# Block-sparse attention with an FFN: gathering the neighbour K blocks beside the sampled ones, and striding the sampled rows over the partitions

## The chip, the cores and the metric

The kernel runs on one core of one Trainium2 chip. The metric is device time in microseconds (us). The engines are named as the profile names them: PE (TensorE, the matmuls), PEld (its weight loads, which overlap PE), DVE (VectorE), ACT (ScalarE), POOL (GpSimd) and SP (SyncE, which here only issues DMAs).

## The reference

Attention over 4 batches, 8 heads, 768 positions and 64 dimensions, with a mask of 24 x 24 blocks of 32 positions, and behind it a feed-forward layer with the activation h - tanh(h):

```python
mask = np.abs(blk_i - blk_j) <= window          # window = 1
mask = mask | (blk_i == 0) | (blk_j == 0) | (blk_i == n_blocks - 1) | (blk_j == n_blocks - 1)
for qb in range(n_blocks):
    for kb in sampled_blocks[qb]:               # 3 drawn blocks for each query block
        mask[qb * block:(qb + 1) * block, kb * block:(kb + 1) * block] = True
scores = np.where(mask, scale * q @ k.T, -1000000000.0)
attn = softmax(scores)
x = (attn @ v) moved to (3072, 512)
out = (h - np.tanh(h)) @ w_out   with   h = x @ w_in
```

Query blocks 0 and 23 see all keys. Each of the 22 others sees eight blocks of keys: itself with its two neighbours (96 keys), the first and the last block (64) and three sampled ones (96). A sampled block that repeats one of the others counts once; the kernel turns the V rows of such a repeat to zeros, so its keys drop out.

## The kernel before

The heads are worked in two passes (`c` = 0 and 1) of four heads. A pass has 30 units: eight for query blocks 0 and 23 (kinds Y and X) and 22 of kind `block`, one for each other query block with its four heads and four batches. 44 block units in all, and they are what the change touches. K and Q of a pass stand turned in SBUF (`kq`): 128 partitions are two heads of 64 dimensions each.

A block unit `n` goes through these steps:

- `gather_k` (lines 207 to 210), on POOL: three copies of 128 partitions x 8 x 32 elements, from columns of `kq` that a register gives (`bass.ds(x, 32)`), into the tile `kr`, whose 160 columns are block 0, three sampled blocks, block 23. The two fixed blocks are put there once a pass (`edges_k`). There are `NKR` = 2 such tiles, so the copies for unit n wait for the scores of unit n - 2.
- `gather_v` (lines 217 to 226), on the SP queue: one DMA of 96 rows for the neighbours into `vw[..][0]`, and three of 32 rows for the sampled blocks into partitions 0:32, 32:64 and 64:96 of `vw[..][1]`; a row is 4,160 bytes. Partitions 96:128 of both hold the fixed blocks (`edges_v`). There are `NVW` = 4 such pairs of tiles; the gather for unit n waits for `accum` of unit n - 4.
- `scores` (lines 231 to 248), on PE: for two halves of the heads, four batches (`q`) and two heads in the rows of the array (`j`), one product of 96 columns straight from `kq` and one of 160 columns from `kr`, so 32 matmuls a unit. In float32 the profile counts each as two matmul instructions with a weight load each.
- `most` on DVE (row maxima), `exps` on ACT, `turn` on PE (8 transposes), `copy` out of PSUM on ACT and DVE, `accum` on PE (32 matmuls of 65 columns with V), `norm` on DVE, and a DMA of the result to DRAM (`xscr`).

What stands when is written out by hand: every step has a time in units (`at(n + 0.3, scores, u)`, line 358), all are sorted by it, and each engine and the SP queue keep that order. The gathers have theirs here:

```python
at(n - NKR + 0.35, gather_k, u)
at(n - NVW + 2.65 if u.i >= NVW else -3.5, gather_v, u)
at(n + 0.3, scores, u)
```

In the first pass the SP queue also carries the K, Q and V of the second (`load_kq` at 9.5, 11.5, 13.5, 15.5, `load_vnat` at 16, 18, 20, 22), in the second the first weights of the FFN. The FFN follows from about 329 us on.

Of the kernel before, what the change touches and what calls it, by code (L numbers as in the profile page):

```python
# [11 lines left out]
F32 = mybir.dt.float32  # L12
# [10 lines left out]
P = 128  # L23
B, H, S, D = 4, 8, 768, 64
NB, BLK = 24, 32
T = S // P
# [17 lines left out]
PRE = sorted(((m, ft) for ft in range(NPRE) for m in "io"), key=lambda w: FIRST[w[1]] + (LAG + 0.5) * (w[0] == "o"))  # L44
STEP = 30
TE = STEP * 2 + 1.9
NVW, NKR, VNAT = 4, 2, T * 260
LOADK, LOADV, PRE0, DPRE = 9.5, 16, 31, 4
X0, X1, STAGE = 44, 52, (54, 54.5, 56, 56.5)
POOLED = range(22)  # L50
# [42 lines left out]
@with_exitstack  # L93
def attention_ffn(ctx, tc, kq, v, samp, w_in, w_out, rows, out):
    nc = tc.nc
    cst = ctx.enter_context(tc.tile_pool(name="cst", bufs=1))
    dpool = ctx.enter_context(tc.tile_pool(name="dpool", bufs=1, space=DRAM))
    xscr = [dpool.tile([P, DM], F32, name=f"xscr{b}") for b in range(NB)]

    ident = cst.tile([P, P], F32, name="ident")  # L100
    make_identity(nc, ident)
    bias = [cst.tile([P, 1], F32, name=f"bias{i}") for i in range(2)]
    for x, val in zip(bias, (QB, THR2)):
        nc.vector.memset(x, val)

    mem = ctx.enter_context(tc.tile_pool(name="mem", bufs=1))
    part = [dpool.tile([P, DM], F32, name=f"part{j}") for j in range(CT)]
    f2 = ctx.enter_context(tc.tile_pool(name="f2", bufs=2))
    px = ctx.enter_context(tc.tile_pool(name="px", bufs=2))
    ffn = FFN(tc, w_in, w_out, xscr, ident, bias, out, f2, part, px)  # L110
    psum = ctx.enter_context(tc.tile_pool(name="psum", bufs=1, space=PSUM))
    banks = [psum.tile([P, 512], F32, name=f"ps{i}") for i in range(8)]
    ffn.banks, ffn.hb, ffn.cv, ffn.xt = banks[:4], banks[4:6], banks[6], banks[7]
    with ExitStack() as actx:
        ffn.nc = InOrder(tc)
        attention(actx, tc, kq, v, samp, w_in, w_out, rows, xscr, ident, banks, mem, px, f2, ffn)
        ffn.nc = InOrder(tc, InOrder.ENGINES[:4])
    with ExitStack() as fctx:
        ffn.rest(fctx)
# [15 lines left out]
def attention(ctx, tc, kq, v, samp, w_in, w_out, rows, xscr, ident, banks, mem, px, f2, ffn):  # L135
    nc = InOrder(tc)
    att = ctx.enter_context(tc.tile_pool(name="att", bufs=1))
# [2 lines left out]
    sbank, tbank, obank = banks[:4], banks[4:6], banks[6:]  # L140

    vw = [[att.tile([P, B, VW // 2], F32, name=f"vw{i}{x}") for x in range(2)] for i in range(NVW)]
    kr = [att.tile([P, H, 160], F32, name=f"kr{i}") for i in range(NKR)]
    wraw = att.tile([P, 1024], I32, name="wraw")
    wtmp = att.tile([P, 256], I32, name="wtmp")
    vnat = [px.tile([P, VNAT], F32, tag=("rawx", "lo")[i // 2], name=f"vnat{i}") for i in range(B)]
# [44 lines left out]
    def values(eng, x, b, top):  # L191
        if b % 4 == 1:
            ins, vals[eng] = tc.nc.values_load_multi_w_load_instructions(
                x[0:1, 3 * b - 3 : min(3 * b + 9, 66)], engines=[eng], min_val=0, max_val=top,
                skip_runtime_bounds_check_because="the samples are clamped into this range on the chip",
            )
            for i in ins:
                tc.keep_in_program_order(i)
        b = 3 * ((b - 1) % 4)
        return vals[eng][b : b + 3]  # L200

    def edges_k(c, i):
        k = kqs[c].rearrange("p b a x s -> p (b a) x s")[:, :, 0, :]
        for b, o in ((0, 0), (NB - 1, 128)):
            nc.gpsimd.tensor_copy(out=kr[i][:, :, o : o + 32], in_=k[:, :, b * 32 : b * 32 + 32])

    def gather_k(u):
        k = kqs[u.c].rearrange("p b a x s -> p (b a) x s")[:, :, 0, :]
        for i, x in enumerate(values(mybir.EngineType.Pool, kx, u.b, S - 32)):
            nc.gpsimd.tensor_copy(out=kr[u.i % NKR][:, :, 32 + 32 * i : 64 + 32 * i], in_=k[:, :, bass.ds(x, 32)])  # L210

    def edges_v(c, i):
        for x in range(2):
            b = (NB - 1) * x
            nc.sync.dma_start(out=vw[i][x][96:P], in_=v[c][32 * b : 32 * b + 32])

    def gather_v(u):
        (wa, ra), src, b = vw[u.i % NVW], v[u.c], u.b
        e = nc.sync
        lo, hi = 32 * (b == 1), 96 - 32 * (b == NB - 2)  # L220
        e.dma_start(out=wa[lo:hi], in_=src[32 * b - 32 + lo : 32 * b - 32 + hi])
        if hi - lo < 96:
            o = 0 if lo else hi
            e.dma_start(out=wa[o : o + 32], in_=src[S : S + 32])
        for i, x in enumerate(values(mybir.EngineType.SP, vx, b, S)):
            e.dma_start(out=ra[32 * i : 32 * i + 32], in_=src[bass.ds(x, 32)])

    mm = lambda o, l, r, start=True, stop=True: nc.tensor.matmul(o, lhsT=l, rhs=r, start=start, stop=stop, skip_group_check=True)
    sbs, ms, nbs, ps, pts = {}, {}, {}, {}, {}
# [1 line left out]
    def scores(u):  # L231
        s = sbs[u.n] = sbank[2 * (u.n % 2) : 2 * (u.n % 2) + 2]
        t = kqs[u.c]
        if u.kind in "XY":
            o, w = (0, 512) if u.kind == "X" else (512, 256)
            parts = [(0, 0, w, slice(o, o + w))]
        else:
            parts = [(h, 256 * h + o, w, None) for h in range(2) for o, w in ((0, 96), (96, 160))]
        for h, o, w, ks in parts:
            for q in range(4):  # L240
                bt, b, p = u.at(q, h)
                for j in range(2):
                    r = slice(64 * j, 64 * j + 64)
                    if w == 160:
                        rhs = kr[u.i % NKR][r, 2 * bt + p]
                    else:
                        rhs = t[r, bt, p, 0, ks or slice(32 * b - 32, 32 * b + 64)]
                    mm(s[j][32 * q : 32 * q + 32, o : o + w], t[r, bt, p, 1, 32 * b : 32 * b + 32], rhs)

    def most(u):  # L250
# [86 lines left out]
    for c in range(2):  # L337
        n = STEP * c
        for bt in range(B):
            for k in "YX":  # L340
                units.append(Unit(len(units), k, c, bt))
        for b in range(1, NB - 1):
            units.append(Unit(len(units), "block", c, b, 22 * c + b - 1))
        if c:
            for bt in range(B):
                at(LOADK + 2 * bt, load_kq, c, bt)
                at(n - STEP + LOADV + 2 * bt, load_vnat, c, bt)
        for i in range(NKR):
            at(n + 6.0 - 2 * (c == 0), edges_k, c, i)
        for i in range(NVW):  # L350
            at(n + 4.5 if c else -4, edges_v, c, i)
    assert len(units) == STEP * 2
    for u in units:
        n = u.n
        if u.kind == "block":
# [3 lines that stand above are left out]
        at(n + 0.65, most, u)  # L359
        if u.kind == "Y":  # L360
            at(n + 2.02, exps, u, 1)
            at(n + 2.04, exps, u, 0)
            at(n + 2.8, turn, u)
            at(n + 2.85, copy, u, 1)
            at(n + 2.86, copy, u, 0)
            at(n + 3.55, accum, u)
            continue
        at(n + 1.1, exps, u, 1)
        at(n + 1.2, exps, u, 0)
        at(n + 2.0, turn, u)  # L370
        at(n + 2.2, copy, u, 1)
        at(n + 2.15, copy, u, 0)
        at(n + 2.6, accum, u)
        at(n + 3.05, norm, u)
# [16 lines left out]
    for k in range(2 * NPRE):  # L391
        t = PRE0 + DPRE * k
# [347 lines left out]
```

## Time and profile before

| | |
|---|---|
| Median of 3 runs | 875.26 us (871.41 to 879.06) |
| The profiled execution, timed | 874.05 us |
| Its span, first to last instruction | 872.3 us |
| Granted TensorE clock over the span, mean | 0.961 |
| PE busy | 755.5 us, 9,440 matmuls |
| PEld busy | 601.9 us, 9,440 weight loads |
| DVE busy | 571.7 us |
| ACT busy | 440.1 us |
| POOL busy | 244.8 us |
| DMA | 82,176 packets, 95.53 MB |

Busy shares are over the whole span. What a change in one stage is worth is read from that stage alone: from the waits that end last there, from the chain of work that ended last, and from the busy times of that stretch. The block units stand at about 37 to 173 us (first pass) and 198 to 329 us (second pass).

### The profile page before, as it was taken

What the parts mean: (1) busy time and instruction counts of PE and PEld (TensorE: products, weight loads), DVE (VectorE), ACT (ScalarE), POOL (GpSimd) and SP (SyncE); (2) the same over time, 40 slices, a digit from 0 to 9 for tenths busy, and PEclk for the clock granted to TensorE, in tenths of its full rate; (3) what the DMA queues carried; (4) which work ended last, traced back from release to release, by engine and by line L of the source; (5) the groups of instructions that cost most, each with busy time, mean ns of one, the idle gap of its engine ahead of it and who ended that gap; (6) DMA issues with size and microseconds to landing.
All of it is one profiled execution on the core that took longest, in us unless ns stands there. A gap on an engine that the chain in (4) does not pass through costs nothing.

```text
span 872.3 us, 23289 instructions
## 1 busy us (share of the span) xinstructions
PE 755.5 (87%) x9440; PEld 601.9 (69%) x9440; DVE 571.7 (66%) x1083; ACT 440.1 (50%) x843; POOL 244.8 (28%) x296
## 2 busy tenths in 40 slices
PE   4676677766677679999999899999999999999996
PEld 2455565545555557878888688888888888888884
DVE  3554455666667558989866676776677667766663
ACT  1442333444444337877765455555555555555543
POOL 0221122022222205777752122222222222222221
PEclk9987878999989899999999999999999999999999
DMA  9879988447968941564202121112111100010001
GB/s 354 233 192 292 277 235 196 132 120 189 246 182 242 246 112 56 159 183 155 95 9 57 21 49 25 26 26 42 30 17 26 44 13 1 1 28 22 1 1 48
DMA packets 82176, 95.53 MB, mean 110 GB/s; under 512 B 43795, under 2 KB 64788, under 8 KB 81172
## 3 DMA queue, kind: packets, MB, share of 16 engines
q1 hardware_dynamic: 81732, 92.99, 39.8%
q8 instruction: 74, 1.21, 0.6%
q10 hardware_dynamic: 336, 1.05, 0.4%
q14 instruction: 34, 0.28, 0.1%
HBM read 80.36 MB, written 13.63 MB: 108 GB/s over the span
## 4 chain that ended last, share of the span: by engine, by line
PE 76%; issue 9%; DVE 7%; SPq 3%; DMA 2%; ACT 2%; DVEq 0%; POOL 0%; ACTq 0%
PE ps L79 76%; SPq L555 3%; DVE m L79 3%; DVE nb L79 1%; DVE pt L79 1%; DMA si<-samp 1%; DVE ps L79 1%; ACT p L79 1%; DMA wraw<-w_in 1%; DMA stage<-w_in 0%; DVE x L79 0%; DVE t L79 0%; DVE s L79 0%; DVE flat L79 0%; DMA xscr<-x 0%
## 5 line engine op out<-in xcount | busy, mean ns | idle before, releaser
L79 POOL TENSOR_TENSOR gl<-t,gh 128x512 fp32r<-128x512 f32 x96 | 124.9, 1301 | 319.3 <-ACT gh L79 304.4
L79 ACT ACTIVATE u<-ps 128x512 f32<-128x512 f32 x96 | 57.6, 600 | 203.1 <-PE ps L79 203.1
L79 ACT ACTIVATE p<-ps,nb 128x256 f32<-128x256 f32 x208 | 89.6, 489 | 104.3 <-DVE nb L79 100.1
L79 DVE TENSOR_REDUCE m<-ps 128x2 f32<-128x512 f32 (+2 forms) x120 | 76.5, 649 | 87.9 <-PE ps L79 85.7
L79 PE MATMUL ps<-flat,wx 128*128 128x512 f32 x504 | 124.3, 395 | 0.8 <-DVE t L79 0.8
L79 POOL COPY kr<-kq 128x256 f32 (+1 forms) x140 | 51.0, 405 | 223.3 <-PE ps L79 197.9
L79 PEld LDWEIGHTS ps<-flat,wx 128*128 128x128 f32 x504 | 94.5, 188 | 23.9 <-DVE t L79 1.2
L79 DVE TENSOR_TENSOR t<-t,ps 128x512 f32<-128x512 f32 x74 | 50.7, 685 | 89.7 <-ACT t L79 89.7
L79 PE MATMUL ps<-kq 64*32 64x96 f32 (+2 forms) x1664 | 59.9, 318 | 53.0 <-issue 30.6
L79 PE MATMUL ps<-wx,gh 128*128 128x512 f32 x336 | 105.3, 394 | 0.0
L79 PE MATMUL ps<-ident,p 128*128 128x128 f32 x448 | 72.3, 309 | 19.4 <-DVE pt L79 8.7
L79 PE MATMUL ps<-flat,gh 128*128 128x512 f32 x288 | 88.9, 390 | 0.0
L79 PE MATMUL ps<-vw,pt 128*32 128x65 f32 x2816 | 60.4, 243 | 25.6 <-issue 21.4
L79 PEld LDWEIGHTS ps<-vw,pt 128*32 128x32 f32 x2816 | 50.9, 123 | 41.6 <-issue 36.7
L79 PEld LDWEIGHTS ps<-ident,p 128*128 128x128 f32 x448 | 56.0, 157 | 30.6 <-issue 12.2
L79 DVE COPY_PREDICATED t<-mk,ps 128x512 f32<-128x512 int32 x96 | 71.3, 742 | 6.7 <-ACT mk L79 0.4
L79 PEld LDWEIGHTS ps<-kq 64*32 64x32 f32 x1664 | 29.4, 116 | 66.4 <-issue 40.1
L79 DVE TENSOR_TENSOR ps<-ps,u 128x512 f32<-128x512 f32 x96 | 66.6, 694 | 12.4 <-ACT hs L79 12.1
L79 PEld LDWEIGHTS ps<-wx,gh 128*128 128x128 f32 x336 | 63.1, 188 | 15.2
L79 DVE SCALAR_TENSOR_TENSOR ps<-qq,ps 128x512 f32<-128x512 f32 x96 | 66.6, 694 | 8.4 <-DVE ps L79 0.9
L79 ACT ACTIVATE pt<-ps 128x512 f32<-128x512 f32 (+1 forms) x60 | 34.1, 569 | 74.7 <-PE ps L79 73.8
L79 PE MATMUL ps<-flat 128*128 128x512 f32 x288 | 69.8, 391 | 1.2 <-ACT pt L79 0.7
(82 smaller groups left out, 1341.4 us busy)
## 6 DMA issues: line engine op xcount, KB each, us to landing
vw<-v SPq DMA_DIRECT2D x152, 130.0 KB, 4.7
vw<-v SPq DMA_DIRECT2D x40, 390.0 KB, 6.5
kq<-kq SPq DMA_DIRECT2D x7, 1536.0 KB, 10.1
stage<-w_in SPq DMA_DIRECT2D x13, 512.0 KB, 3.9
stage<-w_out SPq DMA_DIRECT2D x13, 512.0 KB, 3.5
vnat<-v SPq DMA_DIRECT2D x8, 780.0 KB, 9.8
xscr<-x SPq DMA_DIRECT2D x44, 128.0 KB, 5.1
out<-ob SPq DMA_DIRECT2D x48, 64.0 KB, 1.7
```

Source lines behind the costliest of these rows:

```text
L79: r = f(*args, **kw)
L555: self.nc.sync.dma_start(out=to[:, a], in_=rows[q][:, a])
```

## The change

A block unit has one score product of 256 columns for each head, batch and half, 16 matmuls in place of 32. For it POOL copies the 96 neighbour columns into `kr` as well, which grows to 256 columns in the order of the two `vw` tiles: neighbours, block 0, then the sampled blocks and block 23 dealt out in turn with a step of 4. The V rows of the sampled blocks go to partitions i, i + 4, i + 8 and so on, over all 128 partitions. To make room, there are three pairs of `vw` tiles in place of four, so each V gather stands one unit later in the SP queue.

```diff
-NVW, NKR, VNAT = 4, 2, T * 260
+NVW, NKR, VNAT = 3, 2, T * 260
...
-    kr = [att.tile([P, H, 160], F32, name=f"kr{i}") for i in range(NKR)]
+    kr = [att.tile([P, H, 256], F32, name=f"kr{i}") for i in range(NKR)]
...
     def edges_k(c, i):
...
-        for b, o in ((0, 0), (NB - 1, 128)):
-            nc.gpsimd.tensor_copy(out=kr[i][:, :, o : o + 32], in_=k[:, :, b * 32 : b * 32 + 32])
+        for b, o in ((0, slice(96, 128)), (NB - 1, slice(131, 256, 4))):
+            nc.gpsimd.tensor_copy(out=kr[i][:, :, o], in_=k[:, :, b * 32 : b * 32 + 32])
 
     def gather_k(u):
...
-            nc.gpsimd.tensor_copy(out=kr[u.i % NKR][:, :, 32 + 32 * i : 64 + 32 * i], in_=k[:, :, bass.ds(x, 32)])
+            nc.gpsimd.tensor_copy(out=kr[u.i % NKR][:, :, 128 + i : 253 + i : 4], in_=k[:, :, bass.ds(x, 32)])
+        nc.gpsimd.tensor_copy(out=kr[u.i % NKR][:, :, 0:96], in_=k[:, :, 32 * u.b - 32 : 32 * u.b + 64])
 
     def edges_v(c, i):
...
-            nc.sync.dma_start(out=vw[i][x][96:P], in_=v[c][32 * b : 32 * b + 32])
+            nc.sync.dma_start(out=vw[i][x][3:P:4] if x else vw[i][x][96:P], in_=v[c][32 * b : 32 * b + 32])
...
-            e.dma_start(out=ra[32 * i : 32 * i + 32], in_=src[bass.ds(x, 32)])
+            e.dma_start(out=ra[i : 125 + i : 4], in_=src[bass.ds(x, 32)])
...
-            parts = [(h, 256 * h + o, w, None) for h in range(2) for o, w in ((0, 96), (96, 160))]
+            parts = [(h, 256 * h, 256, None) for h in range(2)]
...
-                    if w == 160:
+                    if u.kind == "block":
                         rhs = kr[u.i % NKR][r, 2 * bt + p]
                     else:
-                        rhs = t[r, bt, p, 0, ks or slice(32 * b - 32, 32 * b + 64)]
+                        rhs = t[r, bt, p, 0, ks]
```

On PE, the scores of a block unit before, where the two kinds of product meet (`ps_111` and `ps_112` are two PSUM banks, one for each head in the rows; `kr_135` one of the two K tiles). The eight products of 96 columns of a half are followed by its eight of 160:

```order
L79 MATMUL ps_111<-kq_144 32x96
L79 MATMUL ps_112<-kq_144 32x96
L79 MATMUL ps_111<-kr_135,kq_144 32x160
L79 MATMUL ps_112<-kr_135,kq_144 32x160
L79 MATMUL ps_111<-kr_135,kq_144 32x160
```

The changed kernel's PE at the same step, from the last rows of the unit before (`ident` marks its transposes) into the scores:

```order
L79 MATMUL ps_115<-vw_127,pt_0_765 32x65 x4
L79 MATMUL ps_114<-ident,p_1_762 128x128 x4
L79 MATMUL ps_113<-ident,p_0_769 128x128 x4
L79 MATMUL ps_111<-kr_133,kq_142 32x256
L79 MATMUL ps_112<-kr_133,kq_142 32x256
```

The products of 96 columns are gone, and all sixteen of a unit read `kr` and have 256 columns; the transposes ahead of them and the products with V around them stand where they stood. PE has 5,408 matmuls in the program in place of 6,112.

On POOL, the copies for the first block units before (`kr_134` and `kr_135` are the two K tiles; an ISA row reads a register):

```order
L79 COPY kr_134<-kq_144 128x8x32
L79 ISA
L79 COPY kr_134<-kq_144 128x8x32
L79 ISA
L79 COPY kr_134<-kq_144 128x8x32
L79 ISA
L79 COPY kr_135<-kq_144 128x8x32
```

And with the change, for the same units:

```order
L79 COPY kr_132<-kq_142 128x8x32
L79 ISA
L79 COPY kr_132<-kq_142 128x8x32
L79 ISA
L79 COPY kr_132<-kq_142 128x8x32
L79 COPY kr_132<-kq_142 128x8x96
L79 ISA
L79 COPY kr_133<-kq_142 128x8x32
```

A fourth copy, three times as long, stands behind the three of each unit.

On the SP queue, the V gathers that are issued ahead of the first unit end before with those of the fourth (`vw_132` and `vw_133` are the fourth pair of tiles, `xscr` the results of query blocks 0 and 23):

```order
L79 DMA vw_131<-v 32x1040
L79 DMA vw_132<-v 96x1040
L79 ISA
L79 DMA vw_133<-v 32x1040
L79 ISA
L79 DMA vw_133<-v 32x1040
L79 ISA
L79 DMA vw_133<-v 32x1040
L79 DMA xscr_60<-x_365 32x128
```

And with the change:

```order
L79 ISA
L79 DMA vw_131<-v 32x1040
L79 ISA
L79 DMA vw_131<-v 32x1040
L79 DMA xscr_60<-x_357 32x128
```

The fourth unit's gather now stands behind the results of query blocks 0 and 23, and every gather after it one unit later than before, behind the same loads. DVE and ACT keep their order.

## Rows read from the trace of the kernel before

**Rows 1.** Stretches: busy us (instructions) of PE, PEld, DVE, ACT, POOL; clock, DMA share, GB/s.

```profile
41.00:125.00 84.00, 57.78 (x1803) 47.08 (x1804) 41.75 (x106) 28.24 (x66) 14.20 (x39) 0.82 0.91 252
125.00:172.50 47.50, 35.96 (x1203) 27.62 (x1204) 27.97 (x72) 19.16 (x44) 6.56 (x18) 0.89 0.69 173
200.00:329.40 129.40, 91.01 (x3061) 72.45 (x3061) 79.89 (x204) 53.45 (x122) 27.20 (x62) 0.91 0.75 198
329.40:872.30 542.90, 531.64 (x2308) 431.01 (x2308) 384.22 (x587) 313.64 (x563) 185.64 (x144) 1.00 0.18 46
```

**Rows 2.** Waits of 0 to 330 us: engine and tile, waited for, total us, times, longest.

```profile
PEld ps L79 <- issue: 105.5, 145, 5.2
PE ps L79 <- issue: 64.2, 30, 5.0
PEld ps L79 <- DMA vw<-v: 1.1, 2, 0.8
```

**Rows 3.** PE in order of time, 92 to 98 us: start, us, what [idle before].

```profile
92.27 0.76 PE L79 MATMUL ps<-vw,pt 128*32 128x65 f32 x36
...
97.42 0.77 PE L79 MATMUL ps<-vw,pt 128*32 128x65 f32 x28 [4.39 <-issue]
```

**Rows 4.** The chain that ended last, 63 to 113 us: start, us, what.

```profile
68.50 2.02 issue
70.52 3.69 PE ps L79 x127
74.21 2.79 issue
...
84.06 4.87 PE ps L79 x127
```

**Rows 5.** The page's DMA queues: kind, packets, MB, share of 16 engines.

```profile
q8 instruction: 74, 1.21, 0.6%
```

**Rows 6.** Two stretches from the end of one stall to that of another, columns of rows 1.

```profile
63.88:111.95 48.07, 31.15 (x889) 24.78 (x889) 21.51 (x52) 13.85 (x32) 7.65 (x21) 0.78 1.01 282
149.76:167.48 17.72, 12.39 (x508) 9.82 (x508) 10.86 (x29) 7.31 (x18) 2.18 (x6) 1.00 0.55 148
```

**Rows 7.** The products with V by stretch: busy us (instructions) of PE and PEld.

```profile
41.00:125.00 84.00, 19.45 (x768) 16.16 (x768) 0.82 0.91 252
125.00:172.50 47.50, 11.31 (x580) 9.59 (x583) 0.89 0.69 173
200.00:329.40 129.40, 28.60 (x1408) 24.24 (x1408) 0.91 0.75 198
```

**Rows 8.** Groups by shape: count, busy us, mean ns, idle before by releaser.

```profile
L79 PE MATMUL ps<-kr,kq 64*32 64x160 f32 x1408 | 55.1, 341 | 6.6 <-issue 6.4
L79 PE MATMUL ps<-kq 64*32 64x96 f32 x1408 | 44.1, 275 | 33.9 <-issue 30.6 <-ACT p L79 3.4
L79 PE MATMUL ps<-kq 64*32 64x256 f32 x128 | 6.2, 449 | 19.1 <-ACT p L79 11.6 <-DMA kq<-kq 7.5
L79 POOL COPY kr<-kq 128x256 f32 x132 | 48.3, 406 | 197.9 <-PE ps L79 197.9
L79 POOL TENSOR_TENSOR gl<-t,gh 128x512 fp32r<-128x512 f32 x96 | 124.9, 1301 | 319.3 <-ACT gh L79 304.4 <-DVE ps L79 8.0 <-issue 6.8
```

**Rows 9.** DMA issues of 60 to 125 us: count, KB each, median us to landing.

```profile
vw<-v SPq DMA_DIRECT2D x11, 390.0 KB, 8.6
vw<-v SPq DMA_DIRECT2D x32, 130.0 KB, 6.9
```

**Rows 10.** V gathers (tile vw), 60 to 125 us, then 200 to 330 us.

```profile
DMA to landing us min/median/max: 2.8/7.4/12.5
...
DMA to landing us min/median/max: 2.9/4.5/9.0
```

**Rows 11.** SP's queue: start, us that the issue of four V gathers takes.

```profile
90.79 7.29 SPq L79 DMA_DIRECT2D vw<-v  x4
...
105.46 3.07 SPq L79 DMA_DIRECT2D vw<-v  x4
```

**Rows 12.** DVE by shape, 200 to 329.4 us.

```profile
L79 DVE TENSOR_REDUCE m<-ps 128x2 f32<-128x512 f32 x43 | 29.5, 685 | 33.0 <-PE ps L79 33.0
```

## The prediction

> **What bounds the kernel now.** Three views settle it, read in this order: busy times by stretch, the waits, and the chain. By stretch [rows 1] the FFN from 329.4 us on is PE's own: 531.64 of 542.90 us busy. The change touches none of it. In the three stretches of block units no engine is full: PE is busy 69, 76 and 70% of them, DVE 50, 59 and 62%, POOL under 22%. So something else sets their time. The waits name it: before 330 us PE sat idle 64.2 us in 30 gaps, its weight loads 105.5 us, for "issue", that is for nothing an engine or a transfer of data would have released, and for V tiles only 1.1 us [rows 2]. One such gap of 4.39 us stands in the middle of a run of 64 equal products, 36 before it and 28 behind [rows 3]: all their data were there.
>
> The chain shows a beat: a stall, 127 matmuls, a stall, 127 matmuls [rows 4]. 127 matmuls and as many weight loads are 254 instructions. The profile lists a DMA queue of kind "instruction" with 74 packets of 1.21 MB / 74 = 16.4 KB [rows 5], and the program's 2 x 9,440 = 18,880 PE instructions over 74 packets are 255 each. So I read the stalls as PE waiting for its next packet of some 255 instructions. In these stretches what a unit costs is the number of its PE instructions, not their work.
>
> How long one packet period lasts goes with the load on the DMA engines. Count the periods as matmuls / 127. From 63.88 to 111.95 us, 889 matmuls are 7 periods of 6.87 us at a DMA share of 1.01; from 149.76 to 167.48, 508 are 4 of 4.43 us at 0.55 [rows 6]. The three stretches lie between [rows 1]: 1,803 / 127 = 14.2 periods of 5.92 us at 0.91; 9.5 of 5.01 at 0.69; 24.1 of 5.37 at 0.75. I use these five points as a scale from share to period.
>
> [...]
>
> **The change, part by part.** *PE instructions.* [...] With 64 products with V a unit, the stretches hold 768 / 64 = 12 units, about 10 (580, the last straddles the edge) and 22 [rows 7]. So 3.0, 2.5 and 5.5 periods go, 11 in all. At unchanged periods that is 3.0 x 5.92 + 2.5 x 5.01 + 5.5 x 5.37 = 17.8 + 12.5 + 29.5 = 59.8 us: the ceiling of this part.
>
> *PE work.* The products lose no columns, only starts: 1,408 of 160 columns keep PE busy 55.1 us and 1,408 of 96 44.1 us; of 256 columns, 128 take 6.2 us, so 1,408 take 68.2 [rows 8]. That is 31.0 us less, 0.70 a unit. In the last stretch PE would be busy 91.0 - 22 x 0.70 = 75.6 us over 24.1 - 5.5 = 18.6 periods, 4.1 us each; in the first 4.4, in the second 4.2. All lie under their periods, so the fetch stays the bound and this part is not added. If the fetch were no bound, these 31 us would be the whole gain.
>
> *DMA.* The same bytes must move in less time, so the share rises and the period with it. DMA time is share x stretch: 76.4, 32.8 and 97 us. For each stretch I solve time = periods left x period(share) on the scale. First: 11.2 x 6.87 = 77 us, at a share of 0.99: a gain of 7. Second: 7.0 x 5.6 = 39 us at 0.84: 8.5. Third: 18.6 x 5.9 = 109.5 us at 0.89: 20. Sum 35.5 us; the other 24 of the ceiling are given back to a busier DMA.
>
> *Sampled V rows.* They go to partitions four apart in place of 32 in a row. No row shows such a write. From below: no change, and nothing in it is more or longer pieces, so I leave out a loss. From above: each such transfer takes half its DMA time. They are half of V's 780 KB a unit, so 22% of the bytes of the first stretch, 47% of the second and 34% of the third (bytes as GB/s x time [rows 1]), and DMA time falls by at most 11, 24 and 17%; the same reckoning then gives 12, 12 and 27.5 us, 51.5 in all. I take a quarter of the way, 39.5 us, since 130 KB in 32 partitions already land sooner (6.9 us) than 390 KB in 96 (8.6) [rows 9].
>
> [...]
>
> *Three V buffers in place of four.* The gather for a unit starts when the products of three units before are done, no longer four. Behind a waiting gather on SP stand the store of the last unit and the loads for the second pass; the products with V wait for the gather. Three units must hold one run of products (1.1 us), the issue of four DMAs (3.07 to 7.29 us [rows 11]) and the last landing. By medians in the first stretch this is 1.1 + 4 + 8.6 = 13.7 us, 4.6 a unit, under the 6.4 that 77 us / 12 leave; in the last 1.1 + 4 + 4.5, 3.2 a unit against 5.0. So I price it at nothing; at worst (7.29 + 12.5 us [rows 10, 11]) it is 7.0 a unit in the first stretch, all of its gain.
>
> *POOL.* The three copies of 256 elements take 406 ns each; the new one has 768. By its nearest row in proportion it is 1.2 us, by the two-input subtraction (1,301 ns for 512) 1.95. The three now write with a step of four; no row shows that. Unchanged, a unit is 2.4 us of POOL, against 260.9 / 44 = 5.9 us a unit now and 5.0 then. POOL waits for PE's scores 197.9 us in all [rows 8], and two tiles give it a unit of lead: hidden. The first unit's copies come behind the first loads as before.
>
> *DVE* keeps its work; 79.89 us of it in the last stretch [rows 1] would fill 73% of 109.5. PE's new pace comes nearest to it: a unit has two reductions of 685 ns there, with PE as releaser [rows 12].
>
> **Sum.** The profiled execution took 874.05 us, 0.1% under the median of 875.26. 874.05 - 39.5 = 834.5; I say 835.
>
> **The rivals.** *The period does not lengthen.* The load may only have lengthened it where 1.5 MB loads stood ahead. For it: only the first stretch has them. Against: five points in one line. It gives 874 - 60 = 814. Chance 0.15.
>
> *V comes late.* With three buffers the first stretch, whose DMA is already full, gains nothing, the last half: 8.5 + 10 gives 855. For it: landings of up to 12.5 us, and full DMA engines. Against: 1.1 us of waits for V now. Chance 0.2.
>
> *The stalls are not counted in instructions*, but belong to something that stands once in each unit, which remains when matmuls go: 866 to 874. Against it: the beat is 127 matmuls, not the 136 of a unit. Chance 0.07. [...]
>
> *Slower: POOL sets the pace.* A write with a step of four elements may cost a multiple. Three strided copies and one of 1.2 us pass the 5.9 us of a unit now from 1.57 us each on, 3.9 times the row. At five times a unit takes 7.3 us, 44 x 1.4 = 62 us more: 936. Against: no sign, the copies being 2.4 us otherwise. Chance 0.08.
>
> **How the numbers follow.** The forecast has 0.5, with a range of its own of 820 to 846 (the two ends of V's spread, 822.5 and 838.5, and some us for V or DVE). The range of 811 to 862 takes in the first two rivals. A measurement here tells about 1% from no change, 866 to 884 us: faster by more 0.83 (forecast and first two rivals, less a little for their tail), within 0.09, slower 0.08.
>
> **What would show it.** Right: about 63 instruction packets in place of 74; stalls still 127 matmuls apart; 104 matmuls a unit in place of 136; periods near 5.6 to 6.9 us with DMA shares near 0.85 to 1.0; the third stretch near 110 us and the first near 75. The V spread: landings of 130 KB sooner than 6.9 and 4.5 us at the same share. Wrong: PE waits for vw of more than 10 us (late V), POOL copies above 1.5 us with PE waiting for kr (the slower rival), stalls gone but units as long (DVE or ACT as the releaser), or periods that stay at 5.4 us while the share rises (first rival).

## The result and the profile after

The changed kernel took 835.25 us (median of 4 runs, 832.62 to 839.33), beside 873.34 us for the kernel before (4 runs): a ratio of 0.956, 95% interval 0.949 to 0.963. The forecast was 835. The profiled execution took 833.99 us, its span is 832.2 us, 40.1 us shorter than before. Ratios, here and below, leave out executions more than 1.5% above the fastest of their kernel; medians do not.

The page of the changed kernel: busy times, the queue of kind instruction [rows 5], and the chain that ended last, by line.

```profile
PE 738.8 (89%) x8032; PEld 575.0 (69%) x8032; DVE 592.8 (71%) x1083; ACT 437.9 (53%) x843; POOL 301.0 (36%) x340
...
q8 instruction: 63, 1.03, 0.5%
...
PE ps L79 73%; DMA vw<-v 3%; DVE m L79 3%; DVE nb L79 3%; DVE pt L79 2%; SPq L556 1%; DMA wraw<-w_out 1%; DMA si<-samp 1%; DVE x L79 1%; DVE ps L79 1%; DMA wraw<-w_in 1%; DVE wtmp L79 1%; DVE rs L79 1%; ACT p L79 1%; SPq L79 0%
```

63 packets in place of 74: the 11 that the forecast took away. PE's own work fell by 755.5 - 738.8 = 16.7 us, much less than the span. The waits of 0 to 330 us of the same run [rows 2]: engine and tile, waited for, total us, times, longest.

```profile
PEld ps L79 <- issue: 59.7, 105, 4.1
PEld ps L79 <- DVE pt L79: 34.9, 33, 2.6
PE ps L79 <- DVE pt L79: 27.6, 24, 3.6
PE ps L79 <- issue: 20.2, 15, 3.9
PE ps L79 <- DMA vw<-v: 2.6, 2, 1.4
```

PE's idle time for "issue" fell from 64.2 to 20.2 us. In its place PE waits 27.6 us for `pt`, the copy out of PSUM on DVE. Before, this wait was 10.0 us:

```profile
PE ps L79 <- DVE pt L79: 10.0, 11, 2.4
```

The stretches of block units [rows 1], cut after about the same unit counts (12, 10 and 22), and the FFN: busy us (instructions) of PE, PEld, DVE, ACT, POOL; clock, DMA share, GB/s.

```profile
41.00:109.00 68.00, 50.31 (x1389) 35.33 (x1389) 49.17 (x105) 27.75 (x66) 32.18 (x56) 0.90 0.88 269
109.00:150.00 41.00, 33.62 (x1008) 23.99 (x1008) 31.81 (x79) 19.42 (x46) 14.48 (x25) 0.96 0.86 255
176.00:290.00 114.00, 85.58 (x2389) 62.08 (x2390) 90.45 (x206) 53.01 (x122) 53.09 (x83) 0.93 0.80 230
290.00:832.20 542.20, 531.48 (x2308) 431.10 (x2307) 384.20 (x587) 313.30 (x562) 185.52 (x144) 1.00 0.18 46
```

The three stretches shrank by 16.0, 6.5 and 15.4 us (the second by about a microsecond more, since the products with V of its last unit start at 172.46 us before, at the edge, and at 148.84 us now, inside it); the FFN has its 542 us as before. The granted clock of the three is higher than before (0.90, 0.96 and 0.93 against 0.82, 0.89 and 0.91); no run tells what that alone gave. DVE is busier in all three although it has the same work. The groups show where that comes from [rows 8]: count, busy us, mean ns, idle before by releaser.

```profile
L79 POOL COPY kr<-kq 128x256 f32 x132 | 74.4, 669 | 101.9 <-PE ps L79 101.9
L79 DVE TENSOR_SCALAR nb<-m 128x2 f32<-128x2 f32 x88 | 63.3, 719 | 3.7
L79 PE MATMUL ps<-kr,kq 64*32 64x256 f32 x1408 | 54.5, 413 | 5.5 <-ACT p L79 2.8 <-issue 2.7
L79 POOL COPY kr<-kq 128x768 f32<-128x768 f32 x44 | 36.7, 833 | 0.0
```

The strided copies of 256 elements take 669 ns in place of 406, the new one of 768 takes 833. The small scaling `nb<-m` on DVE went from this, a row of the kernel before in the same view, to a mean of 719 ns:

```profile
L79 DVE TENSOR_SCALAR nb<-m 128x2 f32<-128x2 f32 x88 | 26.5, 301 | 3.0
```

In order of time one sees it stand (changed kernel; start, us, what):

```profile
102.40 2.31 POOL L79 COPY kr<-kq 128x256 f32 x4 [5.41 <-PE ps L79]
103.09 1.64 DVE L79 TENSOR_SCALAR nb<-m 128x2 f32<-128x2 f32 x1
103.31 1.42 DVE L79 TENSOR_REDUCE m<-ps 128x2 f32<-128x512 f32 x1
104.78 0.17 DVE L79 TENSOR_SCALAR nb<-m 128x2 f32<-128x2 f32 x1
```

POOL's four copies end at 102.40 + 2.31 = 104.71 us, the first `nb` at 104.73; the second, with POOL idle, takes 0.17 us. The reduction behind the first, started at 103.31 us, ends at 104.73 as well.

### The profile page after: what moved, and what is told of

The parts are those of the page before. It is cut to its first block, busy times and chain, and to the rows that moved or that the text cites. A ratio compares the mean times of both kernels' runs of the same rounds, so it can differ in the third digit from the quotient of the medians.

```text
span 832.2 us, 20518 instructions
## 1 busy us (share of the span) xinstructions
PE 738.8 (89%) x8032; PEld 575.0 (69%) x8032; DVE 592.8 (71%) x1083; ACT 437.9 (53%) x843; POOL 301.0 (36%) x340
## 4 chain that ended last, share of the span: by engine, by line
PE 73%; DVE 12%; DMA 6%; issue 5%; ACT 2%; SPq 2%; POOL 0%; DVEq 0%; ACTq 0%; POOLq 0%
PE ps L79 73%; DMA vw<-v 3%; DVE m L79 3%; DVE nb L79 3%; DVE pt L79 2%; SPq L556 1%; DMA wraw<-w_out 1%; DMA si<-samp 1%; DVE x L79 1%; DVE ps L79 1%; DMA wraw<-w_in 1%; DVE wtmp L79 1%; DVE rs L79 1%; ACT p L79 1%; SPq L79 0%
## 5 line engine op out<-in xcount | busy, mean ns | idle before, releaser
L79 POOL COPY kr<-kq 128x256 f32 (+2 forms) x184 | 107.4, 703 | 127.0 <-PE ps L79 101.9
L79 DVE TENSOR_REDUCE m<-ps 128x2 f32<-128x512 f32 (+2 forms) x120 | 97.0, 820 | 38.4 <-PE ps L79 37.8
L79 PE MATMUL ps<-vw,pt 128*32 128x65 f32 x2816 | 56.7, 232 | 37.1 <-DVE pt L79 16.9
L79 PEld LDWEIGHTS ps<-vw,pt 128*32 128x32 f32 x2816 | 47.0, 115 | 60.1 <-DVE pt L79 34.9
L79 PE MATMUL ps<-ident,p 128*128 128x128 f32 x448 | 70.2, 303 | 18.0 <-DVE pt L79 10.7
L79 PEld LDWEIGHTS ps<-ident,p 128*128 128x128 f32 x448 | 54.2, 154 | 29.0 <-issue 10.2
L79 ACT ACTIVATE qq<-u,bias 128x512 f32<-128x512 f32 x96 | 69.9, 728 | 0.0
L79 ACT ACTIVATE mk<-u,bias 128x512 f32<-128x512 f32 x96 | 69.7, 726 | 0.0
L79 PE MATMUL ps<-flat,flat 128*128 128x512 f32 x288 | 69.6, 391 | 0.1
```

Source lines behind the costliest of these rows:

```text
L79: r = f(*args, **kw)
```

## The experiments

Medians stand beside runs of the kernel before on the same chip: 870.35 us for the first four, 871.37 for the next four, 871.40 for the last four. Ratios are to those, with 95% intervals.

**The products cut again.** In the changed kernel:

```diff
-            parts = [(h, 256 * h, 256, None) for h in range(2)]
+            parts = [(h, 256 * h + o, w, None) for h in range(2) for o, w in ((0, 96), (96, 160))]
...
-                        rhs = kr[u.i % NKR][r, 2 * bt + p]
+                        rhs = kr[u.i % NKR][r, 2 * bt + p, o - 256 * h : o - 256 * h + w]
```

> The changed kernel, with each product of 256 columns cut again into 96 and 160, both read from the copied tile: 32 matmuls a unit as before, and nothing else undone. If PE is held by the fetch of its instructions, 64 instructions a unit come back, 11 packets in all (74 in place of 63), and with 5 to 6 us a packet the time goes back by 25 to 45 us, to 860 to 880, with the idle time of PE for issue from 20 back to 50 us or more. If the gain came from the strided V rows or the lighter DMA, the time stays within 828 to 842. If only PE's own work counts, at most 31 us come back and the issue waits stay near 20 us.

Measured: 866.14 us, 0.995 (0.992 to 0.998). Its page, and its waits of 0 to 330 us:

```profile
PE 753.3 (87%) x9440; PEld 598.4 (69%) x9440; DVE 600.3 (69%) x1083; ACT 438.0 (50%) x843; POOL 300.1 (35%) x340
q8 instruction: 74, 1.21, 0.6%
...
PEld ps L79 <- issue: 92.1, 121, 4.9
...
PE ps L79 <- issue: 53.6, 32, 4.7
```

31 us came back with 74 packets and with the idle time for issue. The gain lies in the merged product, not in what stands beside it. By the time alone the 31 us that the expectation allows to PE's own work would fit as well. But PE's busy time rose by 14.5 us only (738.8 to 753.3), and the issue waits came back, which PE's work does not explain; the next run tests it from the other side.

**More work, the same instructions.** In the kernel before:

```diff
+            x = 160 if u.kind == "block" and w == 96 and u.b <= 17 else 0
...
-                        rhs = t[r, bt, p, 0, ks or slice(32 * b - 32, 32 * b + 64)]
-                    mm(s[j][32 * q : 32 * q + 32, o : o + w], t[r, bt, p, 1, 32 * b : 32 * b + 32], rhs)
+                        rhs = t[r, bt, p, 0, ks or slice(32 * b - 32, 32 * b + 64 + x)]
+                    mm(s[j][32 * q : 32 * q + 32, o : o + w + x], t[r, bt, p, 1, 32 * b : 32 * b + 32], rhs)
```

> The kernel before with the same number of instructions and more work in them: for query blocks 1 to 17 of both passes the neighbour product has 256 columns in place of 96 (the 160 that are too many are written over by the product that follows). By the groups of the trace before, 256 columns keep PE busy 48 ns an instruction in place of 31, so 34 units x 32 x 17 ns = 19 us more PE work. If the fetch of instructions sets the pace, it hides in the stalls and the time rises by less than 7 us; if PE's own work sets it, by 15 us or more.

Measured: 876.30 us, 1.006 (1.002 to 1.009), 5 us more (2 to 8 by the interval). Its page, and PE's wait of 0 to 330 us:

```profile
PE 773.4 (88%) x9440; PEld 605.9 (69%) x9440; DVE 571.3 (65%) x1083; ACT 439.2 (50%) x843; POOL 244.0 (28%) x296
...
PE ps L79 <- issue: 53.5, 28, 4.7
```

PE's busy time rose by 17.9 us (755.5 to 773.4), and 10.7 us of that came out of the waits for issue (64.2 to 53.5). Most of the work vanished in the stalls: it was not the bound. Together with the run before, which changed the number of instructions, this shows that the number set the pace.

**No step of four.** The changed kernel with the sampled blocks in a row:

```diff
-        for b, o in ((0, slice(96, 128)), (NB - 1, slice(131, 256, 4))):
+        for b, o in ((0, slice(96, 128)), (NB - 1, slice(224, 256))):
...
-            nc.gpsimd.tensor_copy(out=kr[u.i % NKR][:, :, 128 + i : 253 + i : 4], in_=k[:, :, bass.ds(x, 32)])
+            nc.gpsimd.tensor_copy(out=kr[u.i % NKR][:, :, 128 + 32 * i : 160 + 32 * i], in_=k[:, :, bass.ds(x, 32)])
...
-            nc.sync.dma_start(out=vw[i][x][3:P:4] if x else vw[i][x][96:P], in_=v[c][32 * b : 32 * b + 32])
+            nc.sync.dma_start(out=vw[i][x][96:P], in_=v[c][32 * b : 32 * b + 32])
...
-            e.dma_start(out=ra[i : 125 + i : 4], in_=src[bass.ds(x, 32)])
+            e.dma_start(out=ra[32 * i : 32 * i + 32], in_=src[bass.ds(x, 32)])
```

> The changed kernel without the step of four: sampled K columns and V rows stand block by block, as before, all else as changed. If the spread of the V rows over the partitions lightens the DMA as the forecast took it (4 us, at most 16), the time rises to 839 to 851. If it is worth nothing and the strided writes only make POOL's copies longer (669 ns in place of 406) and with them the wait of the small DVE operation nb, the copies fall back to about 406 ns, nb from 719 ns to 450 to 600, and the time falls to 822 to 833.

Measured: 846.80 us, 0.971 (0.966 to 0.976). The theory of the second half fell: POOL's copies and `nb` did shorten, and yet the kernel is slower. Groups of this run:

```profile
L79 POOL COPY kr<-kq 128x256 f32 x132 | 48.7, 407 | 132.8 <-PE ps L79 132.8
L79 DVE TENSOR_SCALAR nb<-m 128x2 f32<-128x2 f32 x88 | 25.2, 287 | 3.0
```

Its waits of PE, as above:

```profile
PE ps L79 <- DMA vw<-v: 15.3, 7, 5.6
```

Its DMA issues of V (count, KB each, median us to landing):

```profile
vw<-v SPq DMA_DIRECT2D x148, 130.0 KB, 5.9
```

And its chain by line:

```profile
PE ps L79 72%; DMA vw<-v 7%; DVE m L79 4%; DMA wraw<-w_out 1%; DVE nb L79 1%; SPq L556 1%; DVE pt L79 1%; DVE ps L79 1%; DMA si<-samp 1%; DVE x L79 1%; ACT p L79 1%; SPq L79 0%; DVE rs L79 0%; DVE wtmp L79 0%; DVE t L79 0%
```

Without the spread V comes late: 7% of the chain are V's DMAs, and PE waits 15.3 us for them, against 2.6 us in the changed kernel.

**The step of four for V alone**, K block by block:

```diff
-            nc.gpsimd.tensor_copy(out=kr[u.i % NKR][:, :, 128 + i : 253 + i : 4], in_=k[:, :, bass.ds(x, 32)])
+            nc.gpsimd.tensor_copy(out=kr[u.i % NKR][:, :, 128 + 32 * i : 160 + 32 * i], in_=k[:, :, bass.ds(x, 32)])
```

> The changed kernel with V rows dealt out over the partitions, but the sampled K columns left block by block, so POOL writes no step of four; the weights of the sampled keys then meet V rows in another order, which changes the values but not the work. If the strided copies on POOL are what makes nb long (719 ns), nb falls to about 290 ns here with the landings as in the changed kernel, and the time falls to 822 to 832, near the kernel with nb on ACT. If nb is slack, it stays within 832 to 839.

Measured: 834.17 us, 0.959 (0.956 to 0.962). Its group of `nb`, and its DMA issues of V:

```profile
L79 DVE TENSOR_SCALAR nb<-m 128x2 f32<-128x2 f32 x88 | 25.5, 290 | 3.0
```

```profile
vw<-v SPq DMA_DIRECT2D x148, 130.0 KB, 4.8
```

This differs from the run before in where V's rows go (and in the K columns of block 23, written once a pass), and is 1.2% of 871 us, 10 us, faster: the spread of V by itself. Against the changed kernel it differs by K's stride in the sampled blocks alone, and that shows no difference beyond the intervals. So the long `nb` is mostly slack.

**The step of four in the kernel before**, with its four V buffers and 32 products:

```diff
-            nc.gpsimd.tensor_copy(out=kr[u.i % NKR][:, :, 32 + 32 * i : 64 + 32 * i], in_=k[:, :, bass.ds(x, 32)])
+            nc.gpsimd.tensor_copy(out=kr[u.i % NKR][:, :, 32 + i : 157 + i : 4], in_=k[:, :, bass.ds(x, 32)])
...
-            e.dma_start(out=ra[32 * i : 32 * i + 32], in_=src[bass.ds(x, 32)])
+            e.dma_start(out=ra[i : 125 + i : 4], in_=src[bass.ds(x, 32)])
```

> The kernel before with the step of four alone (sampled K columns and V rows dealt out, four V buffers, 32 matmuls a unit). If the spread lightens the DMA, landings of 130 KB come sooner, packet periods shorten and the time falls by 4 to 16 us, to 858 to 870. If it does nothing, 870 to 878; if the strided copies on POOL hold DVE up, 876 to 885.

Measured: 861.93 us, 0.989 (0.987 to 0.992): 9 us by itself. PE waits for no V there; its wait for issue (from 64.2 us), the landings of V (from 4.7 us) and `nb` are:

```profile
PE ps L79 <- issue: 52.1, 30, 3.6
...
vw<-v SPq DMA_DIRECT2D x152, 130.0 KB, 4.2
...
L79 DVE TENSOR_SCALAR nb<-m 128x2 f32<-128x2 f32 x88 | 50.8, 577 | 3.9
```

So the 9 us most likely come by way of lighter DMA (landings 4.7 to 4.2 us) and shorter waits for issue (64.2 to 52.1 us). The kernel with the products cut again has as many products and the same spread and is 4 us slower than this one (0.995 against 0.989), though its PE waits for no V either. What it has besides is the copy of the neighbours on POOL and three V buffers; these two were not told apart with the spread in place.

**Three V buffers in the kernel before.**

```diff
-NVW, NKR, VNAT = 4, 2, T * 260
+NVW, NKR, VNAT = 3, 2, T * 260
```

> The kernel before with three pairs of V tiles in place of four and nothing else. The forecast priced this at nothing, from landings that leave room. If that holds, 868 to 874. If late V rows cost time even at the old pace, 876 to 885, with PE's waits for vw above 5 us and DMA vw in the chain.

Measured: 869.29 us, 0.998 (0.995 to 1.001): nothing, at the old pace.

**The scaling on ACT**, and the same with a fourth tile for the sampled V rows:

```diff
-            nc.vector.tensor_scalar(out=nb[:, j], in0=ms[u.n][:, j], scalar1=-0.125, scalar2=None, op0=ALU.mult)
+            nc.scalar.activation(out=nb[:, j], in_=ms[u.n][:, j], func=AF.Copy, scale=-0.125)
```

> The changed kernel with the scaling nb<-m of the block units on ACT in place of DVE (same values). The theory: nb on DVE takes 719 ns on average in place of 301 because it stands still while POOL copies, and now lies on the chain that ends last; on ACT it would take about 0.2 us each, and the time falls by 8 to 20 us, to 815 to 828. The rival: the long nb is slack under the fetch or the V gathers, and the time stays within 831 to 840.

> The changed kernel with nb on ACT and four tiles for the sampled V rows (three for the neighbours), whose gathers then stand one unit earlier in the SP queue. If late V rows now hold PE (DMA vw is 4% of the chain that ended last), the time falls by 4 to 15 us against the kernel with nb on ACT, to 814 to 826. If the neighbours' rows or the fetch hold it, it stays within 826 to 832.

Measured: 829.29 us, 0.951 (0.947 to 0.955), and 832.98 us, 0.955 (0.952 to 0.959). On ACT `nb` takes 204 ns:

```profile
L79 ACT ACTIVATE nb<-m 128x2 f32<-128x2 f32 x88 | 17.9, 204 | 54.8 <-DVE m L79 54.7
```

The first is the lowest ratio of a kernel that computes the whole, but its interval meets that of the changed kernel, so a gain of about 0.5% is possible and not shown; the two other runs with `nb` on ACT (0.955 here, 0.958 below) do not add to it. The fourth tile, split off from the neighbours' three, gained nothing: its PE waits still longer for V. This wait, a piece of its chain, and the DMA issue with which that piece starts:

```profile
PE ps L79 <- DMA vw<-v: 25.5, 12, 5.2
...
72.52 9.92 DMA vw<-v
...
vw<-v SPq DMA_DIRECT2D x1, 390.0 KB, 9.9
```

It is a gather of the neighbours, 390 KB, and so are 8 of the 11 V gathers in that chain. The neighbours still have three tiles there. So asking earlier for the sampled rows alone does not help; whether four whole pairs would, no run shows.

**Less DMA.** The changed kernel again, then with a third of the sampled V gathers left out, then with the second pass's loads later, then those with `nb` on ACT:

```diff
-            e.dma_start(out=ra[i : 125 + i : 4], in_=src[bass.ds(x, 32)])
+            if i < 2 or u.i < NVW:
+                e.dma_start(out=ra[i : 125 + i : 4], in_=src[bass.ds(x, 32)])
```

```diff
-LOADK, LOADV, PRE0, DPRE = 9.5, 16, 31, 4
+LOADK, LOADV, PRE0, DPRE = 9.5, 24, 31, 4
...
-                at(LOADK + 2 * bt, load_kq, c, bt)
+                at(LOADK + 4 * bt, load_kq, c, bt)
```

> The changed kernel once more, beside the three that follow on one chip: 832 to 840.

> The changed kernel with the third sampled V block of a unit gathered for the first three units alone (later units read old rows there, so values change): 130 of V's 780 KB a unit less, one DMA of four less. If the DMA engines, full in the first pass, now bound it through late V rows, the time falls by 8 to 20 us, most of it before 150 us, and the chain loses its DMA vw share (3%). If the fetch and DVE hold it whatever DMA does, it falls by less than 4 us.

> The changed kernel with the second pass's K and Q loaded every four units in place of two, and its V from unit 24 on in place of 16, so that part of it moves into the stretch of 150 to 176 us, where the DMA share is 0.34. If the DMA bounds the first pass, it falls by 4 to 12 us, to 823 to 831, with a lower share before 111 us. If V or K of the second pass then come late there, it rises to 838 to 848.

> The same late loads together with nb on ACT: if both are worth what their single runs say (4 to 12 and about 5 us) and do not overlap, 815 to 827; if they stand on the same path, no better than the better of the two.

Measured: 838.04 us, 0.961 (0.954 to 0.968); 828.73 us, 0.952 (0.947 to 0.957); 837.54 us, 0.963 (0.957 to 0.968); 837.04 us, 0.958 (0.948 to 0.968). A sixth of V's bytes less gives some 9 us, with the intervals just overlapping, and no V gather is left in its chain by line. The run also takes one of four V issues a unit off the SP queue, so bytes and issues are not told apart. By engine the chain of the changed kernel on this chip:

```profile
PE 69%; DVE 14%; DMA 6%; issue 5%; ACT 2%; SPq 2%; POOL 0%; DVEq 0%; ACTq 0%; POOLq 0%
```

and of the one with a third of the sampled V gathers left out:

```profile
PE 72%; DVE 18%; issue 5%; ACT 2%; SPq 1%; DMA 1%; POOL 0%; DVEq 0%; ACTq 0%; POOLq 0%
```

Loading later gave nothing. Two stretches of the changed kernel on this chip, then the same two of the kernel that loads later, columns as above:

```profile
50.00:110.00 60.00, 45.13 (x1256) 31.08 (x1251) 44.73 (x98) 25.83 (x62) 28.22 (x49) 0.91 0.91 276
110.00:148.00 38.00, 28.51 (x883) 20.14 (x884) 29.11 (x67) 17.42 (x42) 13.86 (x24) 1.00 0.88 255
...
50.00:110.00 60.00, 44.75 (x1280) 31.13 (x1264) 44.65 (x98) 25.62 (x62) 28.82 (x50) 0.91 0.80 236
110.00:148.00 38.00, 27.32 (x792) 19.78 (x792) 24.69 (x61) 15.97 (x39) 13.23 (x23) 0.92 0.93 282
```

The load that was taken from the first stretch (0.91 to 0.80) stands in the second (0.88 to 0.93). The two relief measures together gave no more than one.

## Why the prediction was right, and where two of its terms were not

**The bound before: right.** The stalls went with the number of instructions, which the forecast read as their fetch. Merged products take 11 packets and 44 us of PE's idle time for issue; cutting them again gives 31 us back; 17.9 us of work without instructions cost 5. That a unit gives up a quarter of a packet, which is behind the forecast's 3.0, 2.5 and 5.5 periods, used a round size of a packet that no run shows. The runs show 254 instructions between two stalls, and PE instructions over q8 packets of 18,880 / 74 = 255 before and 16,064 / 63 = 255 now. By these the 32 matmuls and 32 weight loads that a unit loses are a quarter as well, and 44 x 64 / 255 makes 11.04 packets.

**PE's own work: wrong in size, 31.0 us forecast.** PE's busy time fell by 16.7 us. The forecast added the busy times of the products of 160 and of 96 columns (55.1 + 44.1 us), but these groups take turns and their records overlap. The busy time of all that reads `kq` (every score product), 0 to 330 us, before and after:

```profile
0.00:330.00 330.00, 83.31 (x3072) 0.90 0.78 215
...
0.00:330.00 330.00, 70.53 (x1664) 0.94 0.75 225
```

That is 12.8 us less, and the 83.31 us before are less than the 99.2 of those two groups alone. The forecast did not add this term, so its sum is not hurt; the rival of PE's work is weaker than it was put.

**"So the fetch stays the bound": not throughout.** PE's waits for issue fell by 44.0 us and its work by 16.7, together 60.7, about the ceiling of 59.8; the span fell by 40.1, so some 20 us came back. The forecast, too, gave 24 us of the ceiling back, but to packet periods that lengthen on its scale with the DMA share, from 4.43 us at 0.55 to 6.87 at 1.01 [rows 6]. What the changed kernel shows in that place is above all PE's wait for DVE's `pt`, 17.6 us longer than before, a wait that the forecast put at nothing, and 2.6 us for V. From 130 to 138 us the chain of the changed kernel runs through `nb`, and two units (208 matmuls) take 7.36 us without PE waiting for issue; the kernel with `nb` on ACT shows the beat of 127 there:

```profile
130.39 3.26 PE ps L79 x104
...
134.46 1.67 DVE nb L79
...
137.75 3.26 PE ps L79 x104
...
122.32 3.75 PE ps L79 x127
126.07 1.17 issue
127.23 3.72 PE ps L79 x127
```

Taking the one away leaves the other, so DVE and the fetch stand side by side. The scale from DMA share to period does not hold here either: 7.36 us are 4.5 us per 127 matmuls at a DMA share of 0.88, where the scale says 5.8. The two ends of the scale differ in granted clock as well (0.78 and 1.00) [rows 6]; no run separates clock and share.

**The spread of V: right in sign, too small.** "I take a quarter of the way" gave 4 us of a possible 16; the run with V's step alone shows 10, and in the kernel before the step brought 9. The step that failed is the choice of the nearest row: landings of 130 against 390 KB said nothing about which partitions they go to. The upper end, half the DMA time for such a transfer, was the author's assumption, and no run shows it: with V's step alone the median landing of 130 KB went from 5.9 to 4.8 us.

**The merged product without the spread: less than forecast.** It kept 0.029 x 870 = 25 us with its fourth copy and three buffers (run without a step of four), where the forecast had 35.5. "So I price it at nothing" of the three V buffers holds at the old pace (0.998). At the new one, with rows in a row, PE waits 15.3 us for V, and that price was missed. Whether the third buffer or the rate of the DMA makes V late there is not shown: no run has the merged product with four whole pairs.

These two misses, some 10 us too much and 6 too little, nearly cancel; that the sum met the measured time to a microsecond is luck. That fewer PE instructions pay, by tens of microseconds, is not.

**By stretch.** The forecast had gains of 7 to 12, 8.5 to 12 and 20 to 27.5 us. Counted exactly, from the first product with V of one unit to that of another (12, 9 and 21 units), the profiled executions show, in us:

| | first | second | third |
|---|---|---|---|
| Before | 76.8 | 44.3 | 116.8 |
| Changed, without the step of four | 69.3 | 41.2 | 105.2 |
| Changed | 60.9 | 37.7 | 102.7 |

In the first stretch the merged product without the spread gives 7.5 us at a DMA share of 0.97, much as forecast for a full DMA, and the spread gives more than that again. The second and third fall short with and without the spread. In the third the changed kernel's PE does not wait for V at all; it waits 6.4 us for issue (26.5 before) and 11.0 us for `pt` (1.1 before).

**The signs.** 63 packets came, and 104 matmuls a unit. Stalls 127 matmuls apart came only in parts. The third stretch is near its 110 us (114.0), the first well under its 75 (68.0).

**POOL: right that it does not set the pace**, wrong in sizes (669 ns for 406, 833 for 1.2 us), and its effect on DVE was not seen. The slower rival did not come.

What bounds the changed kernel now is not one thing. Fetch, V's arrival and DVE stand so close that relieving any one of them gave at most about 1% (0.961 to 0.952 with a third of the sampled V gathers left out). Whether moving `nb` alone is a gain stays open.

## What to carry to other kernels

Where a matrix engine idles for nothing the profile can name, count instructions between the gaps: a constant count near that of one instruction packet (here 254 beside 255) was the sign that fewer, wider instructions pay more than less work does: 2,816 PE instructions put back, all else as changed, cost 31 us, while 17.9 us more work cost 5 us. Check it with two runs, one that changes the count alone and one that changes the work alone. Do not add the busy times of groups that take turns on one engine: here two came to 99.2 us, and all that reads `kq` to 83.31. When such a bound is lifted, price again each thing that had slack only because of it, buffers and the small operations of other engines alike, and not at the old medians: three V buffers cost nothing at the old pace (0.998), and at the new one, with rows in a row, PE waited 15.3 us for V. A rows-to-partitions layout that costs no byte was worth 1.2% of 871 us here; change it and the product shape in separate runs, or one hides the other.

## What was not expected of the hardware

The scaling `nb<-m` on DVE, 128 x 2 elements in SBUF, took longer beside POOL's copies, and how much longer went with POOL's write. It took 0.17 us with POOL idle. With copies in a row it took 287 to 301 ns on average; with a step of four elements 577 ns (three copies, the kernel before) and 719 ns (four copies, the changed kernel; 861 ns with its products cut again). In the rows shown above it lasted to the end of POOL's whole run (104.73 against 104.71 us). On a write with that step POOL itself took 1.65 times as long (669 against 406 ns).
